# Last pair regrouped, new step orders, k cast in two halves, one combining exponential and maxima in two bf16 parts, in a chunk-selecting attention with a slot mixture of experts

## The chip, the core and the metric

One core of one Trainium2 chip. TensorE (PE, with its weight loads PEld), VectorE (DVE), ScalarE (ACT), GpSimd (POOL) and the DMA queues run side by side, each in its own program order, and wait for each other by semaphores. The metric is device time in microseconds (us), the median of the runs.

## What is computed

Four batches of eight heads, 768 positions, head size 64. Keys lie in 24 chunks of 32. Per query an upper bound for each chunk is formed from the chunk's minimum and maximum of k, the six best causal chunks are kept, and a softmax runs over them. The result, as 3072 rows of 512, goes through a soft mixture of 8 experts with 4 slots each: dispatch weights are a softmax over rows, combining weights a softmax over the 32 slots.

```python
ub = np.sum(np.maximum(q[:, :, :, None, :] * k_min[:, :, None, :, :], q[:, :, :, None, :] * k_max[:, :, None, :, :]), axis=-1)
top_chunks = np.argsort(np.where(causal, ub, -1e9), axis=-1)[..., -6:]
attn = softmax(np.where(mask, scale * q @ k.T, -1e9)) @ v         # cut: (sum + 1e-9), mask = selected and causal
logits = x @ phi
d = softmax(logits, axis=0); slot_input = d.T @ x                 # E = 8, 4 slots each
slot_out[e] = np.maximum(slot_input[e] @ w1[e], 0.0) @ w2[e]
return softmax(logits, axis=1) @ slot_out
```

## The kernel before

Work goes by pairs of heads, 16 pairs (4 per batch). The order is written out by hand: for each pair one string of step names (PLAIN, LOGITS, SLOTS, AFTER by its place in the batch, BEFORE_LAST for pair 14, FINAL for pair 15), and every engine runs its share in that order. Within pair i the steps do work for several pairs:

- `trk`, `trq`, `evk`, `evq`: k and q of pair i+2 are transposed on PE (L238) and copied out on ACT (L247); `kmin`, `kmax`, `bd`, `qsn`, `qsp` make the bound's operands on DVE (L256, L262, L268, L276, L286).
- `ub`, `sel`, `ns`, `evns`: for pair i+1 the bound on PE (L296), its top six by twelve DVE instructions (L317) and a comparison (L320), a small POOL cast (L319), and the selection transposed (L328, L336).
- `sc:g`, `ex:g`, `mk:g`: group g of pair i's scores on PE (L346, and L356 for the selection), the exponential on ACT (L370), the diagonal mask on POOL (L380). The two score buffers in PSUM tie PE to ACT: a third group waits until the first exponential is done.
- `pv`: pair i-1, exponentials times v (L398); `norm`, `xt`, `evx`: pair i-2 is normalised on DVE (L410, L411), transposed on PE (L420) and copied out (L431).
- `moe_*`: for the batch that just ended, logits (L443), a column maximum over rows kept as a running bound (L451 to L478), dispatch (L531), the running slot sums, the combining weights (L516 to L520, three ACT instructions that lay each slot out several times) and their transposes (L554).

Loads of k, q, v and of the experts' weights are cast from f32 to bf16 by DMAs that POOL issues, in POOL's program order: `lkq`, `lv`, `lw`, `lh`. The first pair's k and q alone come as f32 on SP's queue and are cast on DVE (L585). The weights w1 of all experts and w2 of six are loaded along the way; the last two w2 come in eight parts, `lh:0` to `lh:7` (L155), of 256 columns each. Matmuls on constants (`warm`, L229) fill PE's gaps at the start, `keep` (L772) those at the end.

After the pairs come the last batch's logits (L443), the maximum over all rows (L804 to L811), its way back to all partitions (L820, L825), dispatch, the first expert layer (L873), its transposes (L885, L889), and the second layer (L912 for four experts, L937 and L947 for the others). Its output is needed in two halves of 256 columns: half y=1 is finished first, scaled (L992), and multiplied with the combining weights of the first six blocks of 256 rows (L981, scaled by L970 on DVE and L967 on ACT, stored by SP at L983). Then half y=0 is finished (L937, L947 and L1000) and goes the same way; the other six blocks follow with all 512 columns (L1010, stores L1016 and L1014).

Of the kernel before, what the change touches and what calls it, by code (L numbers as in the profile page):

```python
# [59 lines left out]
def kernel(  # L60
# [21 lines left out]
    LAST = NPAIR - 1  # L82

# [36 lines left out]
    pm_pad = static.tile([P, P], F32, name="pm_pad")  # L120
    ns_t = [static.tile([P, NJ, 2, 2, CH], BF16, name=f"ns_t{i}") for i in range(2)]
# [62 lines left out]
    load(1, "k")  # L184
# [31 lines left out]
    )  # L216
    def spread_mask(t0, t1, copy):
# [14 lines left out]
    def transposes(i, nm):  # L232

        ps = p_tp.tile([P, NQT, P], BF16, name="tr_ps", tag="tp")
        src = st.pop((nm, i))
        for g in range(NQT):
            for h in range(2):
                nc.tensor.matmul(  # L238
                    ps[h * 64:(h + 1) * 64, g, :], lhsT=src[:, h, g * D:(g + 1) * D], rhs=ident,
                    is_transpose=True,  # L240
                )
        st[nm + "ps", i] = ps

    def evac_T(i, nm, copy=nc.scalar.copy):

        t = tp3.tile([P, S], BF16, name=nm + "T", tag=nm + "T")
        copy(  # L247
            t.rearrange("d (p g) -> d p g", g=NQT),
            st.pop((nm + "ps", i)).rearrange("d g p -> d p g"),
        )  # L250
        st[nm + "T", i] = t
# [133 lines left out]
    def pv(i, ts):  # L385
        if i == LAST and ts[0] == 0:
            st["at", i] = p_tp.tile([P, 2, 3 * (D + 1)], F32, name="at_ps", tag="tp")
        elif i == LAST and ts[0] == 3:
            st["at", i] = p_sc.tile([P, 2, 512], F32, name="at_ps", tag="sc")
        elif ts[0] == 0:  # L390
            st["at", i] = p_at.tile([P, 2, 512], F32, name="at_ps", tag="at")
        at, tb = st["at", i], 3 if i == LAST and ts[0] > 2 else 0
        for t in ts:
            for h in range(2):
                o = at[:, h, (t - tb) * (D + 1):(t - tb + 1) * (D + 1)]
                for kg in range(t + 1):
                    g, c = (BLOCK_LAST if i == LAST else BLOCK)[(kg, t)]
                    nc.tensor.matmul(  # L398
                        o, lhsT=st["e", i, g][:, h, c:c + P], rhs=v_t[i % NV][:, h, kg, :D + 1],
                        start=(kg == 0), stop=(kg == t),  # L400
                    )
# [32 lines left out]
    def moe_logits(b, hgs=range(NDG), ps=None):  # L434
# [6 lines left out]
        for t in range(NQT):  # L441
            for hg in hgs:
                nc.tensor.matmul(  # L443
                    ps[:, t, :], lhsT=xT[:, hg, t * P:(t + 1) * P], rhs=phi[:, hg],
                    start=(hg == 0 and t == 0), stop=(hg == NDG - 1 and t == NQT - 1),
                )

# [6 lines left out]

    def moe_max(b):

        pmT = p_tp.tile([P, P], F32, name="pmT_ps", tag="tp")
        nc.tensor.matmul(pmT, lhsT=pm_pad, rhs=identf, is_transpose=True)
        st["pmT", b] = pmT

    def moe_bound(b):
# [4 lines left out]
        st["mb", b] = mb  # L466

    def moe_exp(b):
        lg = st.pop(("lg", b))
        bc = p_tp.tile([P, NS], F32, name="bc_ps", tag="tp")  # L470
        nc.tensor.matmul(
            bc, lhsT=st.pop(("mb", b)).broadcast_to([P, P]), rhs=identf[:, :NS], start=True, stop=True,
        )
# [40 lines left out]
    def exp_c(lc):  # L514
        c4 = lc[:, :NQT].rearrange("p t (j s) -> p t j s", s=SPE)
        nc.scalar.activation(c_pad[:, :, :, :SPE], c4[:, :, :4], func=ACT.Exp)  # L516
        pairs = c4[:, :, 4:8]
        pairs = bass.AP(pairs.tensor, pairs.offset, [list(x) for x in pairs.ap[:-1]] + [[1, 2 * SPE]])
        nc.scalar.activation(c_pad[:, :, :, SPE:3 * SPE], pairs, func=ACT.Exp)
        nc.scalar.activation(  # L520
            c_pad[:, :, :, 3 * SPE:4 * SPE], c4[:, :, 4:5].broadcast_to([P, NQT, 4, SPE]), func=ACT.Exp)
# [52 lines left out]
    wplan = {2: 1, 3: 1, 4: 1, 5: 1, 6: 1, 9: 1, 10: 1, 11: 1, 12: 2, 13: 2, 14: 1, 15: 1}  # L574
# [8 lines left out]
    def cast(n, nm, copy):  # L583
        t = ring[nm][0][:, :2]
        copy(t, stage[:, n])  # L585
        st[nm, 0] = t
# [62 lines left out]
    nc.vector.memset(pm_pad, 0.0)  # L649
    qneg(2)  # L650
    qpos(2)

    def step(i, what):
# [47 lines left out]
        else:  # L701
# [11 lines left out]
    LOGITS = """sc:0 trk sc:2 ex:0 ex:2 ub norm sc:3 evk lv mk:0 ex:3 pv:0 pv:5 mk:2 pv:1 sc:1 sel xt trq pv:2:3 ex:1 evq sc:5 ex:5 mk:1 kmin sc:4 evx ns moe_logits@2 lw kmax bd evns mk:3 qsn ex:4 mk:5 mk:4 pv:4 lkq moe_copy@2 qsp"""  # L713
    SLOTS = """sc:0 ex:0 moe_max@3 mk:0 sc:1 ex:1 mk:1 ub moe_bound@3 norm sel trk moe_comb@3 evk sc:2 pv:0 pv:1:2 lkq ex:2 sc:3 moe_exp@3 ex:3 mk:3 trq xt pv:3 kmin mk:2 evqd moe_exp2@3 evx kmax bd moe_scale@3 lw sc:4 ex:4 lv mk:4 sc:5 moe_comb2@3 ex:5 mk:5 ns pv:5:4 evns moe_dispatch@3 qsn qsp"""
# [4 lines left out]
    for i in range(1, NPAIR):  # L719
        if i >= EARLY:  # L720
# [5 lines left out]
        for what in order.split():  # L726
# [3 lines left out]
            if what == "mz":  # L730
                nc.gpsimd.memset(siT_pad, 0.0)
                continue
            if what == "ctc":
                moe_ct_copy(B - 2)
# [9 lines left out]
    BL = B - 1  # L744
    normalise(LAST - 1)
    pv(LAST, [0, 1, 2])
    at_a = st["at", LAST]
    at_b = p_sc.tile([P, 2, 512], F32, name="at_ps", tag="sc")

    def pv_last(blocks, start=False, stop=False):  # L750
        for n, (t, kg) in enumerate(blocks):
            g, c = BLOCK_LAST[(kg, t)]
            for h in range(2):
                nc.tensor.matmul(
                    at_b[:, h, (t - 3) * (D + 1):(t - 2) * (D + 1)],
                    lhsT=st["e", LAST, g][:, h, c:c + P], rhs=v_t[LAST % NV][:, h, kg, :D + 1],
                    start=(start and n == 0), stop=(stop and n == len(blocks) - 1),
                )

    pv_last([(3, 0), (3, 1), (3, 2), (4, 1), (4, 2), (4, 4), (5, 2), (5, 4)], start=True)  # L760
    x_transposes(LAST - 1)
    evac_x(LAST - 1, copy=nc.scalar.copy)
    normalise(LAST, 0, 3, at_a)
    pv_last([(4, 3), (5, 1), (5, 3), (3, 3)])
    pv_last([(4, 0), (5, 0), (5, 5)], stop=True)
    lgt = p_at.tile([P, 2, 512], F32, name="lgt_ps", tag="at")
    lg12 = lgt[:, 0, :2 * NQT * NS].rearrange("p (t o s) -> p t o s", t=NQT, o=2)
    lg1, lg2 = lg12[:, :, 0, :], lg12[:, :, 1, :]
# [5 lines left out]
    h_ps = [p_sc.tile([P, 2, 512], F32, name="h_ps0", tag="sc")]  # L774

    def col_sums(ps, b):
        c = cT_all[:, b * NQT:(b + 1) * NQT].rearrange("p (m a) (c x) -> p m x (a c)", a=2, x=2)
        for n in range(NQT):
            nc.tensor.matmul(
# [269 lines left out]
```

## Time and profile before

| what | us |
|---|---|
| median of 3 runs (158.31 to 158.5) | 158.46 |
| the profiled execution's own time | 158.78 |
| its span, first to last instruction | 157.1 |
| PE, DVE, ACT, POOL busy | 137.4, 121.6, 121.2, 97.8 |
| first score exponential (ACT) starts | 13.15 |
| pair 15's first exponential starts | 117.15 |
| last batch's logits are read by DVE (L804) | 125.88 |
| first expert layer starts (L873) | 129.24 |
| first output store is issued | 138.36 |
| last evacuation ends | 150.08 |

The span holds five stages: a start until some 20 us, in which transfers and one chain of small steps set the pace; fifteen pairs of 6.3 to 9 us; the last pair and the logits; the expert layers; and the output, 6.29 MB of stores. A share of busy time mixes these, so each step below is read from its own stage. Rows of the chain give start, length and what; rows of the timeline add the idle time before in square brackets, and who ended it.

### The profile page before, as it was taken

How to read it: one execution, taken by the hardware profiler on the slowest of the kernel's cores; microseconds unless marked ns; L12 is line 12 of the kernel's file. 1: busy time of each engine (PE TensorE's matmuls, PEld its weight loads, DVE VectorE, ACT ScalarE, POOL GpSimd, SP SyncE). 2: the span in 40 equal slices, each digit the busy share in tenths (PEclk: the TensorE clock that was granted, in tenths of full speed). 3: DMA queues.
4: the chain of work that ended last, by engine and by line, in shares of the span. 5: the costliest groups of instructions: out<-in, count | busy, mean ns of one | idle time of the engine just before them, and what ended most of it. 6: DMA issues, size and time to landing. Idle time of an engine off the chain costs nothing.

```text
span 157.1 us, 6041 instructions
## 1 busy us (share of the span) xinstructions
PE 137.4 (87%) x2485; PEld 91.1 (58%) x2486; DVE 121.6 (77%) x442; ACT 121.2 (77%) x172; POOL 97.8 (62%) x196
## 2 busy tenths in 40 slices
PE   7866799999999999999999999999998999877700
PEld 5543456767666676756657676767666854444200
DVE  4758789889899899999989999989952761178820
ACT  3557899999999988999979789998879531277600
POOL 7899861975878786493868866678598780000000
PEclk9999999999999999999999999999999999999975
DMA  5999999999999999999999999999999999949995
GB/s 152 188 187 211 178 210 213 164 192 215 197 209 196 209 194 211 204 220 172 195 173 211 206 214 177 215 195 214 208 206 212 208 194 197 131 169 384 400 422 230
DMA packets 46171, 33.31 MB, mean 212 GB/s; under 512 B 26304, under 2 KB 41664, under 8 KB 46144
## 3 DMA queue, kind: packets, MB, share of 16 engines
q0 software_dynamic: 41328, 25.86, 113.5%
q1 hardware_dynamic: 4816, 7.08, 12.2%
q8 instruction: 19, 0.31, 0.7%
q14 instruction: 8, 0.07, 0.1%
HBM read 52.49 MB, written 6.29 MB: 374 GB/s over the span
## 4 chain that ended last, share of the span: by engine, by line
PE 58%; DVE 22%; ACT 7%; issue 3%; POOL 3%; DMA 2%; DVEq 0%; POOLq 0%; ACTq 0%
PE at_ps L398 11%; PE sc_ps L346 11%; PE sc_ps L356 8%; PE tr_ps L238 6%; ACT e_sb L370 4%; PE xT_ps L420 3%; PE ub_ps L296 3%; DVE mx L317 3%; DVE x_sb L411 3%; ACT o_sb L967 3%; PE h_ps L873 2%; DVE mm L256 2%; DVE mm L262 2%; DMA w_sb<-in_k_dram 2%; PE ns_ps L328 2%
## 5 line engine op out<-in xcount | busy, mean ns | idle before, releaser
L370 ACT ACTIVATE e_sb<-sc_ps 128x768 bf16<-128x768 f32 (+1 forms) x96 | 83.1, 926 | 6.5 <-PE sc_ps L356 5.1
L380 POOL TENSOR_SCALAR_AFFINE_SELECT e_sb<-e_sb 128x256 bf16<-128x256 bf16 x96 | 37.9, 417 | 22.0 <-ACT e_sb L370 21.8
L346 PE MATMUL sc_ps<-qT,kT 64*128 64x384 bf16 (+3 forms) x258 | 37.5, 308 | 2.3 <-ACT e_sb L370 2.0
L356 PE MATMUL sc_ps<-nsT,smask 64*128 64x384 bf16 (+2 forms) x294 | 37.7, 284 | 0.3
L398 PE MATMUL at_ps<-v_t,e_sb 128*128 128x65 bf16 x642 | 27.1, 194 | 0.4 <-DVE x_sb L411 0.2
L398 PEld LDWEIGHTS <-e_sb 128*128 128x128 bf16 x642 | 22.8, 97 | 6.5 <-POOL e_sb L380 2.9
L317 DVE MAX8 mx<-ub_ps 128x8 f32<-128x8 f32 (+1 forms) x192 | 16.9, 164 | 5.8 <-PE ub_ps L306 4.9
L346 PEld LDWEIGHTS <-kT 64*128 64x128 bf16 x258 | 12.6, 93 | 9.5 <-issue 3.5
L356 PEld LDWEIGHTS <-smask 64*128 64x128 bf16 x294 | 14.7, 95 | 3.8 <-issue 1.3
L169 POOL DMA_DIRECT2D v_t<-in_v_dram x16 | 16.6, 1041 | 0.2
L411 DVE TENSOR_TENSOR x_sb<-at_ps,inv 128x768 bf16<-128x768 f32 (+1 forms) x17 | 15.5, 910 | 0.6
L247 ACT COPY kT<-tr_ps 128x768 bf16<-128x768 bf16 x16 | 12.8, 802 | 3.5 <-PE tr_ps L238 3.5
L256 DVE TENSOR_REDUCE mm<-kT 128x24 bf16<-128x768 bf16 x16 | 15.1, 944 | 0.4 <-ACT kT L247 0.4
L262 DVE TENSOR_REDUCE mm<-kT 128x24 bf16<-128x768 bf16 x16 | 15.1, 943 | 0.0
L247 ACT COPY qT<-tr_ps 128x768 bf16<-128x768 bf16 x14 | 11.5, 823 | 3.3 <-PE tr_ps L238 3.3
L145 POOL DMA_DIRECT2D w_sb<-in_moe_w_dram x14 | 10.2, 729 | 0.0
L296 PEld LDWEIGHTS <-qpn 128*128 128x128 bf16 x192 | 6.0, 96 | 6.7 <-issue 3.3
L431 DVE COPY xT_sb<-xT_ps 128x768 bf16<-128x768 bf16 (+1 forms) x15 | 8.0, 536 | 2.2 <-PE xT_ps L420 2.0
L296 PE MATMUL ub_ps<-bd,qpn 128*128 128x48 bf16 x192 | 7.8, 184 | 1.6 <-POOL qpn L276 1.4
L238 PE MATMUL tr_ps<-ident,k_in 128*64 128x128 bf16 x192 | 8.4, 223 | 0.7 <-DVE k_in L585 0.5
L420 PE MATMUL xT_ps<-ident,x_sb 128*128 128x128 bf16 x96 | 8.2, 220 | 0.3 <-DVE x_sb L411 0.3
L238 PE MATMUL tr_ps<-ident,q_in 128*64 128x128 bf16 x192 | 8.4, 223 | 0.0
(155 smaller groups left out, 216.3 us busy)
## 6 DMA issues: line engine op xcount, KB each, us to landing
w_sb<-in_moe_w_dram POOLq DMA_DIRECT2D x14, 1024.0 KB, 12.7
out_dram<-o_sb SPq DMA_DIRECT2D x14, 256.0 KB, 2.5
v_t<-in_v_dram POOLq DMA_DIRECT2D x16, 192.0 KB, 10.6
k_in<-in_k_dram POOLq DMA_DIRECT2D x7, 384.0 KB, 9.3
q_in<-in_q_dram POOLq DMA_DIRECT2D x7, 384.0 KB, 10.4
out_dram<-o_sb SPq DMA_DIRECT2D x5, 512.0 KB, 4.0
w_half<-in_moe_w_dram POOLq DMA_DIRECT2D x8, 256.0 KB, 11.5
w_sb<-in_k_dram SPq DMA_DIRECT2D x1, 384.0 KB, 3.3
```

What stands on the lines that cost most here:

```text
L238: nc.tensor.matmul(ps[h * 64:(h + 1) * 64, g, :], lhsT=src[:, h, g * D:(g + 1) * D], rhs=ident, is_transpose=True,)
L247: copy(t.rearrange("d (p g) -> d p g", g=NQT), st.pop((nm + "ps", i)).rearrange("d g p -> d p g"),)
L256: nc.vector.tensor_reduce(mm[:, 0, 0, :], kT, axis=AX.X, op=ALU.min)
L262: nc.vector.tensor_reduce(mm[:, 1, 0, :], kT, axis=AX.X, op=ALU.max)
L296: nc.tensor.matmul(o, lhsT=qpn[:, x, t * P:(t + 1) * P], rhs=bd[:, x], start=(t == 0 and x == 0), stop=False,)
L317: nc.vector.max(mx[:, a, :], ub[:, a, :max(8, 4 * t + 4)])
L346: nc.tensor.matmul(ps[:, h, c:c + w], lhsT=kT[r, kg * P:(kg + 1) * P], rhs=qT[r, qs], start=True, stop=False,)
L356: nc.tensor.matmul(ps[:, h, c + (f - t0) * P:c + (l - t0) * P], lhsT=smask[r, x, kg].rearrange("p a b -> p (a b)"), rhs=nsT[r, (f - x * NJ ...
L370: nc.scalar.activation(e[:, :, :w], st.pop(("scps", i, g))[:, :, :w], func=ACT.Exp, scale=scale)
L380: nc.gpsimd.affine_select(out=e[:, :, c:c + P], in_=e[:, :, c:c + P], compare_op=ALU.is_ge, fill=0.0, base=0, pattern=[[0, 2], [1, P]], ch ...
L398: nc.tensor.matmul(o, lhsT=st["e", i, g][:, h, c:c + P], rhs=v_t[i % NV][:, h, kg, :D + 1], start=(kg == 0), stop=(kg == t),)
L411: nc.vector.tensor_tensor(st["x", b][:, t0:t1, 2 * j:2 * j + 2, :].rearrange("p t h d -> p h t d"), at[:, :, :, :D], inv.broadcast_to([P, ...
```

## The change

- Start: only k of pair 0 comes as f32 over SP; its two heads are cast side by side, one on DVE, one on ACT. q of pair 0 is now the first casting load that POOL issues. The transposes of k go to two PSUM tiles, copied out by ACT and DVE. `qneg` of pair 0 moves from POOL to DVE. The loads of q for pairs 2 and 3 and of v move behind four POOL selections; the loads for pairs 4 and 5 move ahead of the first weights, and wait on POOL for transposes of pair 1. Of the 11 `warm` rounds that follow the first 8, 4 remain: 2 behind k's transposes and 2 ahead of `ns`. Three POOL instructions make `once`, from which `live` is formed later.
- Pairs: the column maximum is carried as a high and a low bf16 part (`high`, `moe_lo`, `mb_lo`), each with a matmul of its own in place of one f32 matmul. The combining weights are laid out as sliding windows of 24, so one ACT instruction replaces three.
- Pairs 14 and 15 get new groups and orders; pair 15's row blocks 0 to 2, 3 and 4, and 5 are finished, normalised, transposed and copied out in turn, and the logits taken from them in turn; the column maximum is begun on blocks 0 to 4.
- End: the second layer runs half y=1 for all experts first (256 columns per matmul), then half y=0 for all, so `so_part` falls away.

```diff
-    [(2, 0, 384, 0)],
-    [(4, 0, 256, 0), (2, 384, 128, 256)],
-    [(3, 0, 384, 0), (1, 512, 128, 384)],
-    [(5, 0, 128, 0), (0, 512, 256, 128)],
+    [(4, 0, 256, 0)],
+    [(2, 0, 384, 0), (0, 512, 128, 384)],
+    [(3, 0, 384, 0), (5, 0, 128, 384)],
+    [(0, 640, 128, 0), (1, 512, 128, 128), (2, 384, 128, 256)],
...
-    for n, (nm, src) in enumerate((("k", k), ("q", q))):
-        nc.sync.dma_start(out=stage[:, n], in_=src[0, :2].rearrange("h (p g) d -> p h (g d)", p=P))
+    nc.sync.dma_start(out=stage, in_=k[0, :2].rearrange("h (p g) d -> p h (g d)", p=P))
+    load(0, "q")
...
-        nc.tensor.matmul(pmT, lhsT=pm_pad, rhs=identf, is_transpose=True)
+        nc.tensor.matmul(pmT, lhsT=high(pm_pad), rhs=ident, start=True, stop=False)
+        nc.tensor.matmul(pmT, lhsT=pm_lo, rhs=ident, start=False, stop=True)
...
+        mb_lo = small.tile([P, 1], BF16, name="mb_lo", tag="mb_lo")
+        nc.vector.tensor_tensor(mb_lo, mb, high(mb), op=ALU.subtract)
...
-        nc.scalar.activation(c_pad[:, :, :, :SPE], c4[:, :, :4], func=ACT.Exp)
-        nc.scalar.activation(c_pad[:, :, :, SPE:3 * SPE], pairs, func=ACT.Exp)
-        nc.scalar.activation(
-            c_pad[:, :, :, 3 * SPE:4 * SPE], c4[:, :, 4:5].broadcast_to([P, NQT, 4, SPE]), func=ACT.Exp)
+        nc.scalar.activation(c_pad[:, :, :, :WIN], runs, func=ACT.Exp)
...
-    cast(0, "k", nc.vector.tensor_copy)
-    cast(1, "q", nc.vector.tensor_copy)
+    nc.vector.tensor_copy(k_0[:, 0], stage[:, 0])
+    nc.scalar.copy(k_0[:, 1], stage[:, 1])
     warm(8)
-    transposes(0, "k")
-    evac_T(0, "k")
+    transposes(0, "k", ((0, 3), (3, NQT)))
+    evac_T(0, "k", nc.scalar.copy, nc.vector.tensor_copy)
...
-    qneg(0, nc.gpsimd)
-    load_w(0)
+    qneg(0)
     qpos(0)
+    transposes(1, "k")
+    load(4, "k", 2)
     spread_mask(0, NJ, nc.gpsimd.tensor_copy)
-    warm(2)
-    transposes(1, "k")
-    evac_T(1, "k")
-    warm(2)
-    ubound(0)
-    transposes(1, "q")
-    evac_T(1, "q")
-    spread_mask(NJ, NQT, nc.scalar.copy)
-    select(0)
-    load_v(1)
-    warm(5)
+    evac_T(1, "k")
+    spread_mask(NJ, NQT, nc.scalar.copy)
+    ubound(0)
+    select(0)
+    transposes(1, "q")
+    load(4, "q", 2)
+    load_w(0)
+    evac_T(1, "q")
+    load_v(1)
+    warm(2)
...
-    wplan = {2: 1, 3: 1, 4: 1, 5: 1, 6: 1, 9: 1, 10: 1, 11: 1, 12: 2, 13: 2, 14: 1, 15: 1}
+    wplan = {2: 1, 4: 1, 5: 1, 7: 1, 8: 1, 9: 1, 10: 1, 11: 1, 12: 2, 13: 2, 14: 1, 15: 1}
...
-    BEFORE_LAST = """sc:0 ex:0 moe_max@3 sc:4 ex:4 mk:4 ub norm moe_bound@3 sel moe_comb@3 trk evk sc:2 mk:0 ex:2 pv:0 pv:1 pv:2:3 sc:1 ex:1 trq evq moe_exp@3 mk:2 mk:1 xt kmin kmax bd sc:3 lv evx lw ex:3 moe_exp2@3 moe_scale@3 pv:4 moe_comb2@3 sc:5 ex:5 mk:3 lkq mk:5 ns evns moe_dispatch@3 pv:5 qsp moe_ct3@3 qsn lh:0 lh:1"""
-    FINAL = """sc:0 ex:0 mk:0 lh:2 sc:1 ex:1 mk:1 lh:3 sc:2 norm ctc ex:2 pv:0:1:2 mk:2 sc:3 ex:3 xt mk:3 evx sc:4 ex:4 mz mk:4 pv:4:5:3 sc:5 ex:5 mk:5"""
+    BEFORE_LAST = """norm sc:0 ex:0 moe_max@3 moe_bound@3 sc:2 moe_comb@3 ub ex:2 sc:4 moe_exp@3 mk:2 mk:0 sel lv trk pv:0:2:3:4:5:1 evk lw sc:1 kmin ex:4 trq evqd ex:1 mk:1 kmax moe_exp2@3 sc:3 moe_comb2@3 xt mk:4 ns evx moe_scale@3 sc:5 qsn evns ex:3 ex:5 mk:3 qsp bdp lkq moe_dispatch@3 lh:1 moe_ct3@3 lh:0 mk:5"""
+    FINAL = """sc:1 sc:0 norm sc:2 ex:1 pv:0:2:3:4 mk:1 ctc pv:5:1 sc:3 ex:0 ex:2 xt mk:0 ex:3 norm1 sc:4 lh:2 mk:2 ex:4 mk:3 xt1 evx mk:4 pl:0 sc:5 evx1 pl:1 nl:0 pl:3 xl:0 pl:2 nl:1 lgt el:0 mz pl:4 ex:5 pl:5 lh:3 xl:1 lgl:0 nl:2 cs xl:2 ela:1 inv ela:2 lgl:1 pma lgl:2"""
...
-    nc.vector.tensor_reduce(pm, lg1.rearrange("p t s -> p s t"), axis=AX.X, op=ALU.max)
+    nc.vector.tensor_tensor(pm, pm_a, lg1[:, NQT - 1], op=ALU.max)
...
-    experts_out(0)
+    experts_out(1, 0)
+    shared_out(1, 0)
     hidden_T(1)
-    shared_out(1, 0)
     slot_sums()
-    experts_out(1)
+    experts_out(1, 1)
     shared_out(1, 1)
     last_expert_out(1)
-    nc.scalar.activation(so_sb[1], so_ps[:, HD:], func=ACT.Copy, scale=zinv)
-    nc.scalar.activation(so_part, so_ps[:, :HD], func=ACT.Copy, scale=zinv)
+    nc.scalar.activation(so_sb[1], outs[1], func=ACT.Copy, scale=zinv)
...
-    shared_out(0, 0)
-    shared_out(0, 1)
+    for f in range(2):
+        experts_out(0, f)
+    for f in range(2):
+        shared_out(0, f)
     last_expert_out(0)
-    nc.vector.scalar_tensor_tensor(so_sb[0], so_last, zinv, so_part, op0=ALU.mult, op1=ALU.add)
+    nc.vector.tensor_scalar_mul(so_sb[0], outs[0], zinv)
```

In the step names, `pl:n` is a part of pair 15's product with v, `nl:n`, `xl:n`, `el:n` or `ela:n` its normalisation, transposes and copy (DVE or ACT), `lgt` the logits' share of pairs 12 to 14, `lgl:n` that of pair 15, `pma` the early part of the column maximum, `cs` and `inv` the row sums of the combining weights, `norm1`, `xt1`, `evx1` the same steps for pair 14, `mz` a memset on POOL.

More of the change, by code (lines that the diff above doesn't have):

```diff
@@ L190 @@
         nc.vector.memset(headsel[h * 64:(h + 1) * 64, :, h, :], 1.0)
-    nc.vector.memset(live, 0.0)
     nc.vector.memset(lc_sb[:, NQT], 0.0)
-    for j in range(4):
-        nc.vector.memset(live[j * CH:j * CH + 2 * SPE, :], 1.0)
     nc.vector.memset(identf, 0.0)
+    load(1, "k")
     load(1, "q")
     load(2, "k", 2)
-    load(2, "q", 2)
-    load_v(0)
     nc.gpsimd.affine_select(
@@ L440, in moe_logits @@
         xT = st["xT", b]
-        for t in range(NQT):
+        for t in ts:
             for hg in hgs:
@@ L470, in moe_exp @@
         bc = p_tp.tile([P, NS], F32, name="bc_ps", tag="tp")
-        nc.tensor.matmul(
-            bc, lhsT=st.pop(("mb", b)).broadcast_to([P, P]), rhs=identf[:, :NS], start=True, stop=True,
-        )
+        for n, part in enumerate(st.pop(("mb", b))):
+            nc.tensor.matmul(
+                bc, lhsT=part.broadcast_to([P, P]), rhs=ident[:, :NS], start=(n == 0), stop=(n == 1))
         m_new, m_old = m_run[b % 2], m_run[(b + 1) % 2]
@@ L626 @@
     )
-    load(4, "k", 2)
-    load(4, "q", 2)
     load_w(1)
+    once = static.tile([P, 8], BF16, name="once")
+    nc.gpsimd.memset(once, 1.0)
+    for sign, base in ((1, 0), (-1, SPE - 1)):
+        nc.gpsimd.affine_select(
+            out=once, in_=once, compare_op=ALU.is_ge, fill=0.0, base=base,
+            pattern=[[-sign * HOME, 8]], channel_multiplier=sign,
+        )
     for g in range(5):
@@ L649 @@
     nc.vector.memset(pm_pad, 0.0)
+    nc.vector.memset(pm_lo, 0.0)
     qneg(2)
@@ new lines, with part @@
+    BL = B - 1
+    parts = {}
+    def part(n):
+        if n == 0:
+            if "a" not in parts:
+                parts["a"] = p_tp.tile([P, 2, 3 * (D + 1)], F32, name="at_ps", tag="tp")
+            return parts["a"], 0
+        if n == 1:
+            if "b" not in parts:
+                parts["b"] = p_sc.tile([P, 2, 512], F32, name="at_ps", tag="sc")
+            return parts["b"], 3
+        if "c" not in parts:
+            parts["c"] = p_tp.tile([P, 2, D + 1], F32, name="at_ps", tag="tp")
+        return parts["c"], 5
@@ new lines, in pv_part @@
+    def pv_part(n, blocks, start, stop):
+        at, t0 = part(n)
+        for m, (t, kg) in enumerate(blocks):
+            g, c = BLOCK_LAST[(kg, t)]
+            for h in range(2):
+                nc.tensor.matmul(
+                    at[:, h, (t - t0) * (D + 1):(t - t0 + 1) * (D + 1)],
+                    lhsT=st["e", LAST, g][:, h, c:c + P], rhs=v_t[LAST % NV][:, h, kg, :D + 1],
+                    start=(start and m == 0 and (n == 1 or h == 0)),
+                    stop=(stop and m == len(blocks) - 1 and (n == 1 or h == 1)),
+                )
@@ L719, with col_sums @@
+    def col_sums(ps, b):
+        c = cT_all[:, b * NQT:(b + 1) * NQT].rearrange("p (m a) (c x) -> p m x (a c)", a=2, x=2)
+        for n in range(NQT):
+            nc.tensor.matmul(
+                ps[:, n:n + 1], lhsT=c[:, n // 2, n % 2], rhs=live, start=True, stop=True)
+    inv_a = small.tile([P, BL * NQT], F32, name="inv_a", tag="inv_a")
+    pm_a = small.tile([P, NS], F32, name="pm_a", tag="pm_a")
     for i in range(1, NPAIR):
+        if i == NPB + 1:
+            nc.vector.tensor_reduce(live, once, axis=AX.X, op=ALU.max)
@@ L729 @@
                 continue
[L730 to L734, printed above, removed]
+            if i == LAST and final(what):
                 continue
@@ L742 @@
             siT_pad = pads.tile([P, NDG, E, CH], BF16, name="siT_pad")
[L744 to L768, printed above, removed]
+    lg1, lg2 = st["lg12"][:, :, 0, :], st["lg12"][:, :, 1, :]
     def keep(n):
@@ L772, in keep @@
             nc.tensor.matmul(h_ps[0][:, 1, CH:], lhsT=ident, rhs=w_sb[0][:, CH:512], start=True, stop=True)
[L774 to L779, printed above, removed]
-                ps[:, n:n + 1], lhsT=c[:, n // 2, n % 2], rhs=live, start=True, stop=True)
-    csa = h_ps[0][:, 1, :BL * NQT]
-    inv_a = small.tile([P, BL * NQT], F32, name="inv_a", tag="inv_a")
-    for b in range(BL):
-        col_sums(csa[:, b * NQT:(b + 1) * NQT], b)
-    x_transposes(LAST, 0, 3)
-    evac_x(LAST, 0, 3, nc.scalar.copy)
-    normalise(LAST, 3, NQT, at_b)
-    nc.vector.reciprocal(inv_a, csa)
-    x_transposes(LAST, 3, NQT)
-    evac_x(LAST, 3, NQT)
-    moe_logits(BL, range(NDG - 1), lg12)
-    moe_logits(BL, range(NDG - 1, NDG), lg12)
     i_ctx.close()
```

187 lines of the change are left out of this document (121 added, 66 removed).

## The prediction

> **What bounds the kernel now.** I read the page's slices and its chain that ended last, then busy time by stage, then the timeline at both ends.
>
> ```profile
> DMA  5999999999999999999999999999999999949995
> 4.20:12.70 8.50, 6.25 (x92) 3.99 (x91) 5.67 (x21) 4.65 (x6) 7.70 (x12) 1.00 1.39 184
> 32.80:39.30 6.50, 6.50 (x127) 4.36 (x123) 5.96 (x24) 6.40 (x9) 4.02 (x9) 1.00 1.41 204
> 81.00:90.00 9.00, 8.56 (x171) 5.96 (x171) 8.32 (x29) 7.44 (x13) 8.31 (x17) 1.00 1.22 202
> 117.00:125.50 8.50, 7.55 (x179) 6.05 (x174) 5.03 (x11) 6.45 (x8) 6.86 (x12) 1.00 1.08 212
> 137.00:138.00 1.00, 0.60 (x4) 0.39 (x4) 0.29 (x1) 0.90 (x3) 0.00 (x0) 1.00 0.14 19
> 142.00:143.00 1.00, 0.75 (x5) 0.39 (x4) 1.00 (x3) 0.99 (x3) 0.00 (x0) 1.00 1.08 382
> ```
>
> The stage rows give length, then busy time of PE, PEld, DVE, ACT and POOL, the clock, DMA share and GB/s. A plain pair (32.8 to 39.3) is PE's: busy 6.50 of 6.50. Where the mixture's sums come in (81 to 90), DVE is nearly as full, 8.32 of 9.00. The start leaves PE 2.25 idle, the last pair 0.95. Input runs without a break until some 137, dies to 19 GB/s, and then output sets the pace. So time moves by what the start, the last pair and the first store do; an earlier start passes through the pairs whole, since PE is full there.
>
> **The start.** Chain (start, length) and timeline:
>
> ```profile
> 0.81 3.33 DMA w_sb<-in_k_dram
> 4.17 0.81 DVE k_in L585
> 6.60 0.81 ACT qT L247
> 7.50 2.15 POOL qpn L276
> 9.69 0.47 PE ub_ps L296 x12
> 1.47 0.86 POOL L163 DMA_DIRECT2D k_in<-in_k_dram  x1
> 7.23 0.36 PEld L238 LDWEIGHTS <-k_in 128*64 128x64 bf16 x12 [0.41 <-DMA k_in<-in_k_dram]
> L276 DVE TENSOR_SCALAR qpn<-qT 128x768 bf16<-128x768 bf16 x15 | 5.5, 367 | 0.0
> L284 ACT ACTIVATE qpn<-qT 128x768 bf16<-128x768 bf16 x1 | 0.8, 843 | 0.0
> L431 ACT COPY xT_sb<-xT_ps 128x384 bf16<-128x384 bf16 x1 | 0.5, 478 | 0.2 <-PE xT_ps L420 0.2
> 12.30 0.37 DVE nsT L336
> 13.15 2.65 ACT e_sb L370 x3
> 18.89 0.53 PE L238 MATMUL tr_ps<-ident,q_in 128*64 128x128 bf16 x12
> 22.41 0.53 PE at_ps L398 x14
> ```
>
> Pair 0's bound (9.69) waits for POOL's `qneg`, 2.15. On DVE it costs 0.37, and ACT's `qpos`, 0.84, becomes last. k is there at 4.14; half a cast (0.4 on DVE, about 0.48 on ACT, the row of 384 columns) replaces 0.81, half copies replace one of 0.8, so k's minima begin about 0.7 earlier and DVE is free at about 7.8 rather than 8.5. The new question is q: it was copied to `qT` at 6.60, and now comes as POOL's first casting load. The one such row was issued at 1.47 and PE began on it at 7.23: 5.7 with two f32 transfers ahead. q is issued some 0.66 earlier behind one, so 5.1 to 6.6; I take 5.9, one f32 transfer's second (4.14 to the q cast) off. Then transposes to 6.5, copy to 7.4, `qpos` to 8.25, bound at 8.3: 1.4 earlier. Transposes of pair 1's k stand ahead of it on PE; that load, issued at about 2.0, lands by 7.7 at 5.7, and 0.53 later PE is free: 8.25, a tie.
>
> POOL's queue: the load for pairs 4 and 5 now waits for those transposes, and behind it stand `smask` (0.84) and the cast L319. 8.25 plus an issue of 0.8 plus 0.84 is 9.9; the selection needs it at 11.3 (12.66 less 1.4), L319 at 9.9. So the waits are hidden, by 1.4 and by nothing; a late k costs L319 one for one. The loads moved behind selections (q of pairs 2 and 3 from 3.8 to about 5.6, v) are first read at 18.9 and 22: no cost. `once` adds three small POOL instructions (some 0.5) before masks that pv reads at 22: none. `pm_lo`'s memset adds 0.1 to DVE's chain at 20.7, `live` about 0.1. Start: -1.3; ends 0 (q as late as the row's 7.2, which eats what `qneg` gives) and -1.6 (q at 5.1, where k's chain decides).
>
> **The pairs.** One DVE subtraction is added in each LOGITS pair and one in each pair after it, three of each:
>
> ```profile
> L478 DVE TENSOR_TENSOR m_run<-m_run,bc_ps 128x32 f32<-128x32 f32 x2 | 0.4, 188 | 0.4 <-PE bc_ps L471 0.3
> L894 DVE RECIPROCAL zinv<-z_ps 128x1 f32<-128x1 f32 x1 | 0.2, 169 | 0.5 <-PE z_ps L893 0.5
> L471 PE MATMUL bc_ps<-identf,mb 128*128 128x32 f32 x6 | 1.2, 286 | 0.0
> L519 ACT ACTIVATE c_pad<-lc_sb 128x192 bf16<-128x192 f32 x4 | 1.4, 351 | 0.0
> ```
>
> All exposed it is 3 x (0.19 + 0.17) = 1.1. LOGITS pairs are PE's, so only those in the two DVE-full pairs count, and part of their length overlaps the next: +0.2. Against it, f32 matmuls (L471 takes two passes) become pairs of bf16 ones and three combining exponentials one of 576 columns, about 0.1 less of ACT, which is not the limit here. Ends -0.3 and +0.9. `wplan` moves two weight loads later by a pair or two: no cost, since they are read after 129 and the queue is full either way.
>
> **The last two pairs.**
>
> ```profile
> 122.19 0.81 ACT L370 ACTIVATE e_sb<-sc_ps 128x768 bf16<-128x768 f32 x1 [0.49 <-POOL siT_pad L731]
> 124.17 0.57 DVE x_sb L411
> 125.13 0.73 PE lgt_ps L443 x24
> 125.88 0.37 DVE pm L804
> 126.98 0.56 PE lgt_ps L820 x2
> ```
>
> Before, the last exponential ends at 123.0 and the logits at 125.86: a mask, products, normalisation, transposes and a copy of three blocks. Now only block 5 follows, in a group without a mask: products 0.3, reciprocal and product on 128 columns 0.45, transpose 0.2, copy 0.3, logits 0.15, with handoffs 1.8 in place of 2.9. Yet the new orders put all 42 products of a pair between two score groups, 1.6 at the 14 in 0.53 above, while the two score buffers leave ACT one or two exponentials in hand (2.65 for three, 0.9 each): in pairs 14 and 15 ACT then idles about 1.0, and walking the groups through, the last exponential ends some 0.5 later. PE's own work is unchanged, and 0.95 of idleness is all there is to save. -0.3; ends -1.0 and +0.6. Behind it, `pm` on 32 columns instead of 192 follows `pma` closely (no gain), the f32 matmul L820 (0.56) becomes bf16, and `mneg_lo` (0.17) stands before its second part: -0.2; ends -0.4 and 0.
>
> **The output.**
>
> ```profile
> 133.34 0.86 PE so_ps L912 x16
> 136.28 0.33 PE so_ps L937 x12
> 136.88 0.48 ACT so_all L992
> 140.93 0.49 DVE so_all L1000
> 138.36 0.62 SPq L983 DMA_DIRECT2D out_dram<-o_sb  x1
> 142.45 1.92 SPq L983 DMA_DIRECT2D out_dram<-o_sb  x3
> w_half<-in_moe_w_dram POOLq DMA_DIRECT2D x2, 256.0 KB, 9.9
> 127.41 1.47 POOL L155 DMA_DIRECT2D w_half<-in_moe_w_dram  x2
> ```
>
> Half y=1 loses half of 32 matmuls of 512 columns: at 0.33 for twelve of 256, sixteen take 0.44 rather than 0.86 and 0.98. That is 0.96, but PE now waits about 0.25 for `hidden_T`'s copies, which L937 covered: the first store goes 0.7 earlier. The same 0.9 of matmuls moves between the halves. Six stores at SP's pace (138.36 to 142.45, 4.1) fed the queue until the second half's first tile was ready: it was just in time, 142.4. Now it comes 0.7 earlier and 0.9 plus nothing later, so stores pause about 0.8, and the rest of the 6.29 MB is bound by the DMA (382 GB/s in the row of 142 above). Sum +0.1; ends -0.5 and +0.5. The last of the eight weight parts is the second of the two issues shown, near 128.1, and takes about 10: at 138.2. Half y=0's last matmuls read it some 0.5 ahead of L1000, at 140.4 then and near 139 now: a cover of under 1.
>
> Sum: -1.3 + 0.2 - 0.3 - 0.2 + 0.1 = -1.5 on the profiled 158.78 (span 157.1): 157.3; the median stands 0.32 lower, so 157.0. All ends added, -3.8 to +2.0, hardly come together; the likeliest case's own range is 156.2 to 157.8.
>
> **Rivals.** A: q and the cast of L319 land late, the start gives nothing: 158.46 - 0.2 = 158.3, no change that three runs can tell (0.2%, 0.3 us). For it: POOL's loads took 5.7 and more. Against: the queue is emptier.
>
> B, slower: PE drops to half rate.
>
> ```profile
> 1.13 3.35 PE L229 MATMUL warm_ps<-ones_sq 128*128 128x256 bf16 x16 [1.13 <-DVE ones_sq L175]
> 10.59 1.26 PE L229 MATMUL warm_ps<-ones_sq 128*128 128x256 bf16 x10
> ```
>
> Sixteen took 3.35, 0.21 each; ten later took 1.26, 0.13 each with the last one's tail: PE starts slow and speeds up with work. Four `warm` rounds remain of eleven, and from 5.8 to 10.5 PE has only transposes and the bound. At half rate a score group of 0.67 (two times 0.34 at 64x384) takes 1.34 against ACT's 0.88: over four groups 1.8, with slower bound and transposes 2.2. It decides once it exceeds 1.5, so at three groups or more: 158.46 - 1.5 + 2.2 = 159.2. Against: the stage row's clock reads 1.00 throughout, and PE was idle 2.25 there already. The Trainium skill, page "TensorE: Matmul & The Clock Gate", Part 1, states this rule: after an idle window of about 3.4 us the clock halves; its Part 4 says transposes do not count as busy. The sixteen rows agree with the warm-up; by the full rule the sum would be +0.7 instead of -1.5.
>
> C: the last pair's idle time goes whole (-1.0) and the halves overlap (-0.5): 157.0 - 0.7 - 0.6 = 155.7. For it: logits taken in turn. Against: ACT's gaps above.
>
> **Chances.** Forecast 0.56, A 0.14, B 0.14, C 0.16. Faster by over 0.2%: forecast, C and a little of A, 0.75; same 0.1; slower 0.15. Range 155.7 (C) to 158.7 (A, with the pairs' additions a little dearer); B's most is left out.
>
> **What would show it.** First exponential at 11.7 to 12.0 and the bound at 8.3 to 8.5; `qneg` about 0.4 on DVE; pair 15's first exponential near 116; logits read near 124.5; first store near 136.0, a pause of 0.8 before the seventh; last store's end 1.5 earlier. A bound after 9.3, score groups over 0.9 on PE before 20, a pair 14 or 15 over 0.5 longer, or no pause would make it wrong.

## The result, and the profile after

Median 159.37 us of 20 runs, against 158.88 us of 20 runs of the kernel before beside them: ratio 1.0044, 95% interval 1.0022 to 1.0065. It is a little slower; 157.0 was forecast, 155.7 to 158.7 the range. The ratio, here and below, is estimated from fast runs alone and is not the quotient of the two medians, which here is 1.0031. The profiled execution took 159.57 (before: 158.78), its span is 157.9 (157.1).

The page of the kernel after, slices of 3.95 us: TensorE's clock in tenths, and what the DMA engines moved; then the second row for the kernel before (slices of 3.93 us).

```profile
PEclk9987999999999999999999999999999999999995
GB/s 113 152 168 190 215 190 213 171 197 211 163 195 207 194 220 195 154 178 186 198 204 208 200 216 200 193 196 214 216 196 215 216 194 197 193 291 329 371 408 225
```

```profile
GB/s 152 188 187 211 178 210 213 164 192 215 197 209 196 209 194 211 204 220 172 195 173 211 206 214 177 215 195 214 208 206 212 208 194 197 131 169 384 400 422 230
```

Three things stand there that the kernel before did not have: a clock below 9 in the third and fourth slices; stores that begin while input still runs, so that the rate doesn't dip before them (193, 291 instead of 131, 169); and lower rates while only stores are left (329, 371, 408 instead of 384, 400, 422).

Its timeline at the start, at the last pair and at the output (start, length):

```profile
8.17 0.53 PE L239 MATMUL tr_ps<-ident,k_in 128*64 128x128 bf16 x12 [0.92 <-DMA k_in<-in_k_dram]
8.67 0.79 PE L298 MATMUL ub_ps<-bd,qpn 128*128 128x48 bf16 x12
10.44 0.99 PE L228 MATMUL warm_ps<-ones_sq 128*128 128x256 bf16 x4
11.40 0.48 PE L330 MATMUL ns_ps<-ident,ns_t 128*128 128x128 bf16 x3
11.81 0.61 PE L348 MATMUL sc_ps<-qT,kT 64*128 64x512 bf16 x2
12.97 1.94 ACT L372 ACTIVATE e_sb<-sc_ps 128x1024 bf16<-128x1024 f32 x2 [1.62 <-PE sc_ps L358]
...
118.28 1.44 PE L396 MATMUL at_ps<-v_t,e_sb 128*128 128x65 bf16 x42
119.65 0.34 PE L348 MATMUL sc_ps<-qT,kT 64*128 64x384 bf16 x2
120.64 1.94 ACT L372 ACTIVATE e_sb<-sc_ps 128x1024 bf16<-128x1024 f32 x2 [1.35 <-PE sc_ps L358]
...
126.17 0.19 DVE L855 TENSOR_TENSOR pm<-pm_a,lgt_ps 128x32 f32<-128x32 f32 x1 [0.28 <-PE lgt_ps L441]
129.19 2.77 PE L923 MATMUL h_ps<-w_sb,siT_pad 128*32 128x512 bf16 x48 [0.17 <-DVE siT_pad L899]
137.40 9.09 SPq L1036 DMA_DIRECT2D out_dram<-o_sb  x12
```

The bound starts at 8.67, 1.02 earlier than before; but four warm matmuls then take 0.99 instead of 0.61, a score group 0.61 instead of 0.39, and the first exponential is only 0.18 earlier. In the last pair all 42 products of pair 14 stand between two score groups, and ACT idles 1.35. The first store is 0.96 earlier, and the span still ends 0.8 later. In parts, against the forecast; the third column is an experiment below, the same kernel with one tile widened, in whose profiled execution the clock rose earlier and did not drop (us, ends of the stages from the rows above and their like):

| stage | forecast | after | `a6_align` |
|---|---|---|---|
| start, to the first exponential (13.15 / 12.97 / 12.03) | -1.3 | -0.18 | -1.12 |
| on to pair 14's first exponential (109.81 / 109.67 / 108.78) | +0.2 | +0.04 | +0.09 |
| on to the reading of the logits (125.88 / 126.17 / 125.29) | -0.3 | +0.43 | +0.44 |
| on to the first expert layer (129.24 / 129.19 / 128.31) | -0.2 | -0.34 | -0.34 |
| on to the first store (138.36 / 137.40 / 136.52) | -0.7 | -0.91 | -0.91 |
| first store to the end of the span (157.07 / 157.86 / 155.91) | +0.8 | +1.75 | +0.68 |
| sum | -1.5 | +0.79 | -1.16 |

### The profile page after: what moved, and what is told of

It is laid out like the page before. It is cut to its first block, busy times and chain, and to the rows that moved or that the text cites. A ratio compares the mean times of both kernels' runs of the same rounds, so it can differ in the third digit from the quotient of the medians.

```text
span 157.9 us, 6088 instructions
## 1 busy us (share of the span) xinstructions
PE 137.9 (87%) x2509; PEld 92.1 (58%) x2510; DVE 122.4 (78%) x451; ACT 120.4 (76%) x164; POOL 96.3 (61%) x197
## 3 DMA queue, kind: packets, MB, share of 16 engines
HBM read 52.49 MB, written 6.29 MB: 372 GB/s over the span
## 4 chain that ended last, share of the span: by engine, by line
PE 53%; DVE 15%; DMA 11%; ACT 7%; POOL 5%; issue 3%; DVEq 0%; POOLq 0%; ACTq 0%
PE sc_ps L348 12%; PE at_ps L396 12%; PE sc_ps L358 9%; DMA w_half<-in_moe_w_dram 7%; PE tr_ps L239 6%; ACT e_sb L372 5%; DMA q_in<-in_q_dram 4%; PE xT_ps L418 3%; PE ub_ps L298 3%; PE ns_ps L330 2%; DVE mx L319 2%; DVE o_sb L1023 2%; DVE x_sb L409 2%; POOL w_half L157 2%; POOL hT_pad L848 1%
## 5 line engine op out<-in xcount | busy, mean ns | idle before, releaser
L372 ACT ACTIVATE e_sb<-sc_ps 128x768 bf16<-128x768 f32 (+2 forms) x96 | 83.2, 928 | 7.6 <-PE sc_ps L358 6.7
L348 PE MATMUL sc_ps<-qT,kT 64*128 64x384 bf16 (+3 forms) x260 | 38.1, 310 | 1.7 <-ACT e_sb L372 1.5
L358 PE MATMUL sc_ps<-nsT,smask 64*128 64x384 bf16 (+2 forms) x296 | 38.3, 287 | 0.2 <-DVE nsT L338 0.2
L396 PE MATMUL at_ps<-v_t,e_sb 128*128 128x65 bf16 x630 | 26.1, 193 | 0.3 <-DVE x_sb L409 0.2
L396 PEld LDWEIGHTS <-e_sb 128*128 128x128 bf16 x630 | 22.1, 97 | 5.4 <-issue 2.3
L348 PEld LDWEIGHTS <-kT 64*128 64x128 bf16 x260 | 13.2, 94 | 9.1 <-issue 3.0
L409 DVE TENSOR_TENSOR x_sb<-at_ps,inv 128x768 bf16<-128x768 f32 (+3 forms) x18 | 15.6, 869 | 0.6
L249 ACT COPY kT<-tr_ps 128x768 bf16<-128x768 bf16 (+1 forms) x16 | 12.7, 792 | 0.8 <-PE tr_ps L239 0.8
L429 DVE COPY xT_sb<-xT_ps 128x768 bf16<-128x768 bf16 (+1 forms) x16 | 8.6, 537 | 1.2 <-PE xT_ps L418 1.2
L239 PEld LDWEIGHTS <-k_in 128*64 128x64 bf16 x192 | 6.1, 113 | 4.0 <-issue 2.3
```

Of the source, the lines that this page charges most:

```text
L239: nc.tensor.matmul(ps[h * 64:(h + 1) * 64, g - g0, :], lhsT=src[:, h, g * D:(g + 1) * D], rhs=ident, is_transpose=True,)
L249: copy(t.rearrange("d (p g) -> d p g", g=NQT)[:, :, g0:g1], ps.rearrange("d g p -> d p g"),)
L348: nc.tensor.matmul(ps[:, h, c:c + w], lhsT=kT[r, kg * P:(kg + 1) * P], rhs=qT[r, qs], start=True, stop=False,)
L358: nc.tensor.matmul(ps[:, h, c + (f - t0) * P:c + (l - t0) * P], lhsT=smask[r, x, kg].rearrange("p a b -> p (a b)"), rhs=nsT[r, (f - x * NJ ...
L372: nc.scalar.activation(e[:, :, :w], st.pop(("scps", i, g))[:, :, :w], func=ACT.Exp, scale=scale)
L396: nc.tensor.matmul(o, lhsT=st["e", i, g][:, h, c:c + P], rhs=v_t[i % NV][:, h, kg, :D + 1], start=(kg == 0), stop=(kg == t),)
```

## The experiments

All ratios are to the kernel before, run beside each on the same chip.

**First theories: input late (I), chain late (C), clock (H).** The last `w_half` part landed at 140.7 instead of 138.2, so I suspected the new load plan; the rivals were PE's clock in the head and the slow last pair.

```profile
129.36 11.38 DMA w_half<-in_moe_w_dram
```

(From the chain of the kernel after: that transfer, 11.38 long, released the second half.) Four runs, one edit each:

```diff
-    wplan = {2: 1, 4: 1, 5: 1, 7: 1, 8: 1, 9: 1, ...
+    wplan = {2: 1, 3: 1, 4: 1, 5: 1, 6: 1, 9: 1, ...       # a1_wplan
...
+    warm(2)                                                # a2_warm
     transposes(1, "k")
...
     ubound(0)
+    warm(1)                                                # a2_warm
...
-  pv:0:2:3:4 mk:1 ctc pv:5:1 sc:3 ex:0                     # FINAL
+  pv:0:2:3 mk:1 sc:3 ctc pv:4 pv:5:1 ex:0                  # a3_split
...
-    experts_out(1, 0); shared_out(1, 0); hidden_T(1)       # a4_tail: the second layer
+    experts_out(0); hidden_T(1); shared_out(1, 0)          # as before, both halves at once
```

> The changed kernel with the old plan of expert weight loads (pairs 3 and 6 load one again, pairs 7 and 8 none). Theory I, the input queue: the new plan left the queue short near 40 and 64 us, so its last bytes come at 140.2 instead of 138.1; then the last w_half part lands by about 139, the stores of the first halves no longer share the engines with it, and the time falls by 0.8 to 1.5 from 159.37, to about 158.2. Theory C, the compute chain (head and last pair too slow, the second halves late on PE): so_all of the second halves moves by at most 0.3, the time stays within 0.3 of 159.37.

1.0079 (1.0048 to 1.0109). Input did end earlier, its last bytes at 138.3, and nothing was gained: theory I is out. The second halves' `so_all` stayed at 141.12, as theory C has it, but the median came 0.67 above 159.37 and not within 0.3. What the old plan costs in the changed kernel, PE's waits from 14 to 125 us show; the kernels before and after have no such rows there.

```profile
PE at_ps L396 <- DMA v_t<-in_v_dram: 0.4, 1, 0.4
PE tr_ps L239 <- DMA k_in<-in_k_dram: 0.3, 1, 0.3
```

The weights are asked for earlier, and PE waits 0.7 for v and k; that the weights, going ahead of these in the queue, cause it is inferred from POOL's order. The interval overlaps that of the kernel after.

> The changed kernel with three more warm rounds on PE in the head: two ahead of the transposes of pair 1's k, one behind the bound. Theory H, the clock: the granted clock stays 1.00 between 8 and 14 us, score groups of the first pair take 0.39 and 0.34 again, the first exponential starts at 12.4 to 12.6 instead of 12.97. What that is worth at the end: 0.3 to 0.5 if the end follows the chain of the pairs (159.0), nothing if the end follows the input queue (159.4).

1.0058 (1.0026 to 1.0089). The mechanism was right (clock 1.00 throughout, scores at full speed, first exponential 12.23), the time was not: the median span fell from 157.65 to 157.3, but the time outside it rose from 1.73 to 1.90 in the median and 2.89 at most. In its trace a 16 KB block of instructions is fetched from 158.1 to 159.6, after the last store; it is the 20th, every other trace has 19 and none there. The only edit is twelve instructions more on PE, so these most likely pushed the program into another block.

> The changed kernel with score group 3 of the last pair put in the middle of pair 14's value products instead of behind all of them. The 1.35 us that ScalarE is idle before 120.64 shrink to 0.4 or less, the last exponential ends near 122.9 instead of 123.73, the logits are read near 125.4 instead of 126.17. Theory C: the time falls by 0.5 to 0.8, to 158.7. Theory I: the chain waits for the last w_half part all the same, and the time stays within 0.3 of 159.37.

1.0047 (1.0020 to 1.0074), and the chain got worse: from pair 15's first exponential to the last one's end 7.10, after 6.86, before 5.85. ACT's gap before group 3 shrank to 0.56, and two of 0.49 and 0.76 opened behind it: a miss.

> The changed kernel with the second layer's old order: the rows of four experts for both halves at once, then the first stores. The first store is issued near 138.4 instead of 137.40, the second halves' so_all stays near 141, since the last w_half part lands at 139 to 140.7 either way. Theory I: time within 0.4 of 159.37, since the same bytes leave through the same engines and only the stretch in which both streams overlap shrinks. Theory C, with the first halves deciding: 0.7 to 1.0 slower, 160.2.

1.0060 (1.0028 to 1.0092). Here the clock did not drop: first exponential at 11.83, first expert layer at 128.26, last evacuation done at 149.70, 0.38 ahead of before. And the span ended 0.90 behind it, at 157.97. From the last evacuation to the end it is 8.27, before 6.99, after 7.59. So what is left over sits in the stores themselves, whichever order feeds them.

**The stores.** In the trace's packet records a store's packets of 1024 bytes took 46 ns each in the kernel before, all alike; in the kernel after 49 in the mean, a tenth of them 53 or more; those of 4096 bytes 159 and 165. The built program's table of addresses shows a difference: the output tiles `o_sb` start at a multiple of 256 bytes in a partition before, and 224 past one after. The small new tiles ahead of them (`once`, 16 bytes) moved everything behind, the `w_half` tiles too, but the store packets are timed by themselves, and in the windows below no load runs any more. The Trainium skill, page "DMA: Bandwidth & Descriptors", section "How a descriptor splits into AXI transactions", says that a descriptor which does not start at a multiple of 256 bytes fetches from the one below and pays for the unused bytes.

```diff
-    once = static.tile([P, 8], BF16, name="once")
+    once_pad = static.tile([P, 32], BF16, name="once")     # a6_align, a7, a8; 96 columns in a10, a11
+    once = once_pad[:, :8]
...
+    nudge = static.tile([P, 112], BF16, name="nudge")      # b2_shift224: kernel before
+    nudge = static.tile([P, 64], BF16, name="nudge")       # b3_shift128: kernel before
...
-            for x in range(2):                             # a7_align_warm: warm, and three rounds more
-                nc.tensor.matmul(warm_ps[:, 2 * x:2 * x + 2], lhsT=ones_sq, rhs=r[:, :2], ...)
+            nc.tensor.matmul(warm_ps, lhsT=ones_sq, rhs=r, ...)
```

> The changed kernel with the new tile once made 64 bytes wide instead of 16 (only its first 16 are used), so that the tiles behind it, the twelve output tiles among them, start at a multiple of 256 bytes in a partition again, as in the kernel before; in the changed kernel they start 224 bytes past one. Theory A, the address: output packets of 1024 bytes take 46 ns each again instead of 49 in the mean, those of 4096 bytes 159 instead of 165; 3.15 MB leave at 0.384 MB per us instead of 0.345, 3.15 MB at 0.42 instead of 0.405, and the time falls by 0.9 to 1.2 from 159.37, to 158.3. Theory I or C (input stream, chain): packets and time as in the changed kernel.

0.9970 (0.9937 to 1.0003), 158.40 beside 158.80, against 1.0044 (1.0022 to 1.0065) for the kernel after: 0.7% from 48 bytes. Packets are 46 and 159 ns again.

> The kernel before with an unused tile of 224 bytes put ahead, so that its output tiles start 224 bytes past a multiple of 256, as in the changed kernel. Theory A: output packets 49 and 165 ns in the mean, the stretch from the first store to the end of the span grows from 18.7 us to 19.6 or more, time 0.6 to 1.2 above before. Otherwise: no change.

1.0075 (1.0041 to 1.0109). The kernel before, with nothing changed but an unused tile and a memset of its first 8 columns, is as slow as the changed one or slower: first store at 138.19 (0.17 earlier), span 158.03; the stretch between grew from 18.71 to 19.84.

> The kernel before with an unused tile of 128 bytes put ahead: output tiles 128 bytes past a multiple of 256, yet at a multiple of 64 and of 128. If only a start off a multiple of 64 bytes costs, packets stay at 46 and 159 ns and the time stays. If every start off a multiple of 256 costs, packets take longer and the time rises by 0.3 to 1.2. The Trainium skill, page "DMA: Bandwidth & Descriptors", section "How a descriptor splits into AXI transactions", says the second: 36 beats for 1024 bytes from 128, against 32 from 0 and 39 from 224.

1.0070 (1.0041 to 1.0099), packets 49 and 165: a multiple of 128 doesn't do. Windows 143 to 146 of the kernels after, a6_align, b2_shift224, b3_shift128 and before, in this order (length, busy PE, PEld, DVE, ACT, POOL, clock, DMA share, GB/s):

```profile
143.00:146.00 3.00, 1.81 (x14) 0.98 (x12) 2.77 (x6) 2.19 (x5) 0.00 (x0) 1.00 0.97 321
```

```profile
143.00:146.00 3.00, 1.88 (x18) 1.04 (x18) 2.17 (x6) 1.62 (x4) 0.00 (x0) 1.00 1.09 383
```

```profile
143.00:146.00 3.00, 1.84 (x19) 1.17 (x19) 2.43 (x5) 1.82 (x5) 0.00 (x0) 1.00 1.04 343
```

```profile
143.00:146.00 3.00, 1.79 (x19) 1.13 (x19) 2.48 (x5) 1.87 (x5) 0.00 (x0) 1.00 1.02 342
```

```profile
143.00:146.00 3.00, 1.72 (x17) 1.00 (x16) 2.60 (x6) 2.00 (x5) 0.00 (x0) 1.00 1.09 383
```

383 with tiles at a multiple of 256, 321 to 343 without; packets grew by 6% from 224 and from 128 alike, and the rate fell by 10% (343 and 342). By that section of the Trainium skill an estimate gives 39 beats of 32 bytes for 1024 bytes from 224, 36 from 128 and 32 from 0. The direction agrees; the difference between 224 and 128 is not seen here.

> The wide once, and three more warm rounds in the head; each warm round is one matmul of 512 columns instead of two of 256, so that PE has fewer instructions than in the changed kernel and not more (the run with three rounds of two fetched one more 16 KB block of instructions after the last work, from 158.1 to 159.6). Theories A and H together: output packets as in a6_align, granted clock 1.00 through the head, first exponential at 11.9 to 12.5, time 0.4 to 0.8 below a6_align: 157.5 to 158.0, below the kernel before.

0.9947 (0.9921 to 0.9974), 158.39 beside 158.80: faster than the kernel before, but 0.4 above the range expected. Its clocks still spread down to 0.967; executions at 0.98 or more took 157.74 in the median, those at 0.97 or less 158.45.

**The clock, and the last pair.**

```diff
+    warm(3)                                                # a8_align_warm5, a11: rounds of 512 columns
     transposes(1, "k")
...
     ubound(0)
+    warm(2)
...
     # a10, a11: GROUPS_LAST, BEFORE_LAST, FINAL, value products and logits as in the kernel before
...
-    warm(2)                                                # b4_cold: the kernel before
     transposes(1, "k")
     evac_T(1, "k")
-    warm(2)
...
-    warm(5)
+    warm(2)
     ns_transposes(0)
```

> The kernel before with the warm rounds of its head taken away as the change does: none around the transposes of pair 1's k, two instead of five ahead of the selection's transposes. Theory H: in half the executions or more the granted clock falls to 0.5 for 3.4 or 6.8 us from about 10 us on, the mean clocks spread from 0.957 to 0.985 as in the changed kernel, and the median rises by 0.3 to 0.8. If the clock drops for another reason of the changed head, the clocks stay at 0.98.

1.0030 (1.0006 to 1.0053). Taking the rounds from the kernel before makes its clock fall as the change does: mean clock 0.966 in the median of 12 executions (before: 0.984 of 32), nine of them at 0.972 or less. Windows of b4_cold, of the kernel after and of a6_align:

```profile
10.50:14.00 3.50, 2.76 (x21) 1.25 (x20) 2.88 (x11) 2.29 (x3) 3.36 (x6) 0.69 1.65 197
14.00:18.00 4.00, 3.65 (x39) 2.00 (x39) 1.52 (x8) 3.69 (x5) 3.08 (x7) 0.50 1.22 201
```

```profile
10.50:14.00 3.50, 3.29 (x23) 1.56 (x22) 2.63 (x6) 1.83 (x3) 3.31 (x6) 0.51 1.69 184
```

```profile
10.50:14.00 3.50, 1.98 (x21) 0.98 (x22) 2.96 (x6) 2.13 (x4) 3.24 (x5) 1.00 1.72 185
```

The head of a6_align is that of the kernel after; in its profiled execution the clock held. Not all of the 0.94 between their first exponentials (12.97, 12.03) is the drop, as two rows of each show, first the kernel after:

```profile
6.39 0.85 PE L239 MATMUL tr_ps<-ident,q_in 128*64 128x128 bf16 x12
9.54 1.06 DVE L319 MAX8 mx<-ub_ps 128x8 f32<-128x8 f32 x12 [0.83 <-PE ub_ps L308]
```

```profile
6.30 0.53 PE L239 MATMUL tr_ps<-ident,q_in 128*64 128x128 bf16 x12 [0.53 <-DMA q_in<-in_q_dram]
9.12 1.06 DVE L319 MAX8 mx<-ub_ps 128x8 f32<-128x8 f32 x12 [0.68 <-PE ub_ps L308]
```

When the selection begins, before the drop, 0.42 is lost already: the clock first rose at 7.11 instead of 4.79, and q's transposes ran slow. From there to the first exponential it is 2.91 in a6_align, a4_tail, a10_oldlast, a2_warm and the kernel before, where the clock held, and 3.43 in the kernel after, 3.27 in a3_split, 3.21 in b4_cold, where it fell: the drop itself takes 0.3 to 0.5. The trace's clock records change at steps of 3.41 us, and where these fall differs from one execution to the next: 7.11, 10.52 and 13.94 in the profile after, 4.79 in that of a6_align.

> The changed kernel with the wide once and five more warm rounds of one matmul of 512 columns: three ahead of the transposes of pair 1's k, where PE waits for the transfer, two behind the bound. Theory H: the stretch of 3.41 us that sets the clock for the head's scores always holds over 1.4 us of matmuls that are not transposes, so that the clock stays 1.00 in nearly every execution; the median falls by 0.2 to 0.5 against a7_align_warm and the clocks of the executions gather at 0.98. If the rounds delay the bound or the second pair's transposes instead, nothing is gained.

0.9970 (0.9949 to 0.9990), 158.07 beside 158.83; the clocks lie at 0.984 in the median, with three of twelve still at 0.97 or less; against a7_align_warm nothing is gained that the intervals could show. In its profile the first exponential comes at 12.41 and not at 12.03, and the rounds are not the cause: the clock rises at 6.90 here, and the selection begins at 9.45; in a3_split, without them, it rises at 6.94, and the selection begins at 9.46; in a6_align at 4.79 and 9.12. How early the clock first rises differs between executions too, and is worth some 0.3 to 0.4.

> The changed kernel with the wide once and the last two pairs as they were: old groups, old orders, value products, logits and their maximum in one piece; the head, the bf16 maxima, the one exponential and the new order of the second layer stay. Theory L, that the regrouping costs: from the first exponential of pair 14 to the reading of the logits 16.1 us instead of 16.5, first store 0.3 to 0.4 earlier, time 0.2 to 0.4 below a6_align. If the regrouping gains what the prediction gave it (0.3), the time is 0.3 above a6_align.

0.9942 (0.9913 to 0.9971), 157.95 beside 158.83. Its interval overlaps that of a6_align, so the time doesn't settle it; the traces do: from pair 14's first exponential to the reading of the logits 16.21 (a6_align 16.51, before 16.07), on to the first expert layer 3.19 (3.02, 3.36). The regrouping loses 0.30 in the pairs, gets 0.17 back in the shorter maximum and costs 0.13 on the whole, less than the 0.3 that I expected.

> Both: the wide once, five warm rounds and the last two pairs as they were. By theories A, H and L this is the fastest of all, 157.2 to 157.6.

0.9950 (0.9927 to 0.9973), 157.77 beside 158.83, no clock under 0.979; 157.2 to 157.6 was expected. With a7_align_warm, a8_align_warm5 and a10_oldlast it is one of four versions whose intervals lie below 1, and so below that of the kernel after; the intervals don't tell them apart.

## Why the prediction was wrong

- The output (+0.1 forecast, +0.84 in the profile after) is the step that failed in all five profiles with tiles at 224 (the kernel after and the first four runs, packets 49 and 165): "the rest of the 6.29 MB is bound by the DMA (382 GB/s in the row of 142 above)". Bound by it, yes, but I carried the rate over from before, and it fell to some 343. That is worth 0.7% either way (a6_align, b2_shift224). With the rate restored the stage gives -0.91 + 0.68, -0.23; I had +0.1. The 0.68 lies near the 0.8 of the pause by luck: in a6_align the pause before the seventh store is 0.24, and the second store, with loads still running, takes 1.21 to issue instead of 0.55.
- The start (-1.3 forecast, -0.18 in the profile after): right as a chain, wrong about the clock. Where the clock had risen by 4.8 and held, the first exponential came at 11.77 (a10_oldlast), 11.83 (a4_tail) and 12.03, forecast 11.7 to 12.0; where it rose later and held, at 12.19 to 12.41. In the profile after it came at 12.97: 0.42 of the 0.94 is the late first rise, which the forecast had at nothing, and 0.52 is rival B's mechanism; that taking the rounds away causes such a drop, b4_cold shows, and with five put back neither profile has it (a8_align_warm5, a11_oldlast_warm5). I set B aside because the clock read 1.00 throughout; that showed only that eleven rounds were enough. B's 159.2 came near the measured time by luck: with a quarter of the 2.2 that I gave it, and by the stores.
- The last two pairs: -0.3 forecast, +0.43 measured. The gap that I foresaw is there (1.35 by the row, 1.0 taken). From pair 14's first exponential to the end of the last one the pairs are 0.87 longer (14.06, before 13.19), where I had 0.5; and the rest behind it, mis-sized most, takes 2.44 (before 2.86) where I had 1.8. Part of that is PE, still on the logits of pairs 12 to 14 when the last exponential ends at 123.73, so that block 5's products start at 124.12:

```profile
122.92 0.81 ACT L372 ACTIVATE e_sb<-sc_ps 128x768 bf16<-128x768 f32 x1 [0.33 <-PE sc_ps L358]
123.60 0.69 PE L441 MATMUL lgt_ps<-phi_sb,xT_sb 128*128 128x64 bf16 x18
124.12 0.47 PE L748 MATMUL at_ps<-v_t,e_sb 128*128 128x65 bf16 x10
```

  Most of the +0.43 the regrouping does (0.30 by a10_oldlast); 0.14 remain with the old pairs (16.21 against 16.07) and stay open.
- The logits' chain -0.34 (forecast -0.2), the pairs +0.04 to +0.09 (+0.2), and the first store -0.91 (-0.7) came out about as worked out. The pause before the seventh store, 0.75 in the kernel after (forecast 0.8), is in part a wait for the late `w_half` part.
- `wplan` at no cost: right in time, but not for the reason given. The queue was not "full either way": input ended 2.1 later. In the changed kernel the new plan spares k and v a wait of 0.7, and the late end of input cost nothing that a1_wplan could win back.
- Rival A's late loads were not the cause: with the same loads a6_align's start gains 1.12. Rival C did not come: neither idle time nor overlap was won.

## What to carry to other kernels

A new tile of a few bytes moves every tile allocated behind it: compare the start addresses of all tiles that DMAs read, modulo 256, before trusting a rate carried over from an older profile. Where an edit removes matmuls that only keep PE busy, look at the matmuls that are left in every 3.4 us, and compare mean clocks over many executions rather than in one profile; no count of them in these profiles separates the stretches behind which the clock fell from those behind which it held. When a stage is bound by stores, what is won upstream shows as an earlier first store, and the rate of the stores decides what is left of it at the end.

## What was not expected of the hardware

- A store whose SBUF tile starts 128 or 224 bytes past a multiple of 256 runs at 342 GB/s instead of 383.
- The clock halved without PE being idle: in the kernel after, the 3.41 us before the drop hold 1.86 us of PE work, 0.77 of it matmuls that are not transposes; in b4_cold 1.63 and 1.12. The kernel before has 1.35 or more in each such stretch of its head and held 1.00. Yet a6_align held 1.00 through a stretch with 0.61, a10_oldlast through one with 0.77, so the threshold stays open. The Trainium skill, page "TensorE: Matmul & The Clock Gate", Part 1, calls the window free-running, which agrees with the shifting steps; it names an idle window as the cause, which these rows do not bear out word for word.
- A program with one more 16 KB block of instructions, fetched after its last store, spent 1.90 us outside the span instead of 1.73, up to 2.89 (a2_warm, the one version that had it).
